# V rows of one head weighted and folded by VectorE, and an indirect load of 45 rows, in a float32 decode-attention kernel

## The chip, the cores and the metric

The kernel runs on 1 core of one Trainium2 chip. The metric is the device time in microseconds (us) of one execution; shown are the median of several runs and, for one profiled execution, the span from its first to its last instruction.

## The reference

One token's output is a gated mix of two attention blocks over caches of 8192 positions, all in float32: A with 16 heads of K and V, B with 16 query heads that share 8 heads of K and V.

```python
def _A_ref(x, k_cache, v_cache, wq, wo):          # x (1, 1, 448); caches (1, 16, 8192, 256)
    q = (x @ wq).reshape(B, Sq, 16, 256).transpose(0, 2, 1, 3)
    scores = einsum("bhqd,bhkd->bhqk", q, k_cache) * 256 ** -0.5
    o = einsum("bhqk,bhkd->bhqd", softmax(scores), v_cache)
    return o.transpose(0, 2, 1, 3).reshape(B, Sq, 16 * 256) @ wo
# _B_ref: the same, with caches (1, 8, 8192, 256), each head of which serves two query heads
g = sigmoid((x * gate_w).sum(-1, keepdims=True))
return g * _A_ref(...) + (1 - g) * _B_ref(...)
```

The caches are 402 MB of the 433 MB that are read, and each element is used once or twice.

## The kernel before

**The stream.** Everything but one part of one weight matrix is laid out ahead of time in the order of use as one stream in device memory, and SyncE loads it in 54 fills (called loads here, counted from 0) into a ring of three slots of 128 partitions x 15,936 floats. A usual load is one DMA of 15,872 columns, 7936 KB; pieces (tiles of K and V, weights) may be cut at a load's end and go on in the next. A load into a slot is issued when all readers of what stood in it are done, three loads before. `plan()` writes the order, `piece()` runs the code of each piece, and a recorder (`Seq`, whose lines 154 and 155 issue every instruction, so that nearly every row of the profile says L155) puts the instructions on their engines in the order written, with semaphore waits worked out from what overlaps.

**Sets, units, tiles.** The work is 8 sets of three units: unit (s, 2) is KV head s of B with its two query heads, (s, 0) and (s, 1) are two heads of A. Each unit has four tiles (t = 0 to 3) of 2048 positions: 128 partitions x 16 rows x 256. In the stream the V of a tile stands three K tiles after its own K (`LEAD`). So V of (s, 0) stands between K tiles of (s, 1). The query weights of set s + 1 (`wq`) come after the first of these V tiles, and the output weights of the set before (`wo`) among the first V tiles.

**Scores.** For (s, 1) and (s, 2), TensorE multiplies K against the query (`scores`, tile `sc`), VectorE takes the minimum `mn` and transposes the exponentials that ScalarE makes (`px` to `pr`). For (s, 0), K stands by rows, and VectorE does it (`scores_by_row`, the units in `BY_ROW`): a product with the query in place (`slot<-slot,qa`), a sum over each row (`sr<-slot`), the minimum over blocks of partitions (`mn`, `mt`, `st`), ScalarE's exponentials `pxr`, and then a product with `cols` that spreads the 16 weights of each partition into columns for TensorE (`pr<-pxr,cols`, line 519).

**Values.** `attend` multiplies on TensorE, two rows of V a call with 512 result columns, eight calls a tile, into a PSUM tile `o` that holds the unit's sums. `take` brings `o` to SBUF after the unit's last V tile (ScalarE and VectorE, tile `ob`), `project_o` selects the heads, and `emit_set` multiplies by `wo` into `Y`.

**Order by ticks.** `tick()` runs after each K tile and calls what is due: `gather`, `combine` (the softmax's correction factors, through a matmul into `T`, then VectorE and ScalarE, tiles `mnr`, `ew`, `es`, `z`, `rz`, `wr`), `column` (tile `sel`), `spread` (the next set's queries, `qb` and `qa`), `project_o`. All engines work in the order in which this is written.

**The indirect load.** For set 4 (`SIDE_SET`) the query weights do not all come in the stream. `SB` = 472 of B's 512 columns, for the first 384 inputs, are loaded by GpSimd's indirect DMA into the front of the slot of load 23 (`SIDE_FILL`), on 39 partitions only: `SIDE_SHARE` says how many rows each DMA engine carries, engine e serving partitions 64 * (e // 8) + 32 * h + 4 * (e % 8) + i with h in (0, 1) and i in 0 to 3. The rest of the columns (`SREST`) comes in the stream as the piece `ws`. `project_side` uses both.

Of the kernel before, what the change touches and what calls it, by code (L numbers as in the profile page):

```python
# [207 lines left out]
WQ = (4 * KF + 2) * DH  # L208
UNITS = [2, 0, 1]
BY_ROW = {(s, 0) for s in range(NS)}  # L210
KEEP = {(3, 12): 3}
LAST_CUT = [10, 6]
HEAD_AT = {2: 0, 0: 2, 1: 3}
# [2 lines left out]

SIDE_SET = 4
SIDE_FILL = 23
SIDE_SHARE = {0: 6, 2: 6, 7: 6, 8: 6, 15: 6, 4: 5, 1: 4}
SIDE_ROWS = sorted(p for e, n in SIDE_SHARE.items()  # L220
                   for p in [64 * (e // 8) + 32 * h + 4 * (e % 8) + i for h in range(2) for i in range(4)][:n])
SC8 = -(-KF * P // len(SIDE_ROWS))
SB = 472
SREST = 2 * DH - SB + 2 * DH
SIDE = SC8 * SB
XG = 2 * (KF + 1) + SC8
SLOT = 15936
# [55 lines left out]
def gated_decode_attention_kernel(  # L283
# [127 lines left out]
    ST, PR, O, GS, WR, SEL, OB, OC = ({} for _ in range(8))  # L411

    QR, SC, QA = {}, {}, {}

    def project(s, c0, w):

# [16 lines left out]
    def project_side(s, view, far):  # L433

        q = ps_s.tile([2 * BLK, 2 * DH], F32, name="sm")
        near = view[:, :KF * SREST].rearrange("p (c n) -> p c n", c=KF)
        rest = view[:, KF * SREST:]
        for a in range(2):
            nc.tensor.matmul(q[BLK * a:BLK * (a + 1), :], xz[:, KF + a, :], rest, start=True, stop=False,
                             skip_group_check=True)  # L440
        for c in range(KF):
            nc.tensor.matmul(q[0:BLK, SB:], xz[:, c, :], near[:, c, :2 * DH - SB], start=False, stop=(c == KF - 1),
                             skip_group_check=True)
            nc.tensor.matmul(q[BLK:2 * BLK, :], xz[:, c, :], near[:, c, 2 * DH - SB:], start=False, stop=(c == KF - 1),
                             skip_group_check=True)
        for c in range(SC8):
            nc.tensor.matmul(q[0:1, :SB], x8[:, c:c + 1], far[:, c * SB:(c + 1) * SB], start=False, stop=(c == SC8 - 1),
                             skip_group_check=True)
        copy_out(s, q)
# [46 lines left out]
    def scores_by_row(u, t, j0, kt):  # L496

        if t == 0 and j0 == 0:
            ST[u] = small.tile([P, 2, NT], F32, name="st", bufs=4)
        st = ST[u]  # L500
        n = kt.shape[1]
        nc.vector.tensor_tensor(kt, kt, QA[u][:, None, :].to_broadcast([P, n, DH]), op=OP.mult)
        if j0 == 0:
            SC[u, t] = small.tile([P, ROWS], F32, name="sr")
        sc = SC[u, t]
        nc.vector.tensor_reduce(sc[:, j0:j0 + n], kt, axis=AX.X, op=OP.add)
        if j0 + n < ROWS:
            return
        mn = small.tile([P, 1], F32, name="mn")
        nc.vector.tensor_reduce(mn, sc, axis=AX.X, op=OP.min)  # L510
        mt = small.tile([P, BLK], F32, name="mt")
        nc.vector.transpose(mt, mn.to_broadcast([P, BLK]))
        nc.vector.tensor_reduce(st[:, 0, t:t + 1], mt, axis=AX.X, op=OP.min)
        px = small.tile([P, ROWS // 2, 2], F32, name="pxr")
        nc.scalar.activation(px.rearrange("p q k -> p (q k)"), sc, AF.Exp, bias=st[:, 0, t:t + 1], scale=-1.0,
                             accum_out=st[:, 1, t:t + 1])
        pr = small.tile([P, NB * BLK], F32, name="pr", bufs=LEAD + 2)[:, :ROWS * NG * NT].rearrange(
            "p (q c k) -> p q c k", c=NG * NT, k=2)
        nc.vector.tensor_tensor(
            pr, px[:, :, None, :].to_broadcast([P, ROWS // 2, NG * NT, 2]),  # L520
            cols[:, t].rearrange("p g r -> p (g r)")[:, None, :, None].to_broadcast([P, ROWS // 2, NG * NT, 2]), op=OP.mult)
        PR[u, t] = pr.rearrange("p q c k -> p q (c k)")

    def attend(u, t, j0, n, vt):

        w = 2 * NG * R[heads(u)]
        if t == 0 and j0 == 0:
            O[u] = ps_o.tile([P, 2 * DH], F32, name="o")
        pr = PR[u, t]
        for j in range(j0, j0 + n, 2):  # L530
            g = j // 2 % (P // w)
            nc.tensor.matmul(O[u][w * g:w * (g + 1), :], pr[:, j // 2, :w], vt[:, j - j0:j - j0 + 2, :],
                             start=(t == 0 and j < 2 * P // w), stop=(t == NT - 1 and j >= NB - 2 * P // w),
                             skip_group_check=True)

    def take(u):

        o = O.pop(u)
        ob1 = small.tile([P, DH], F32, name="ob1", bufs=1)
        OB[u] = small.tile([P, DH], F32, name="ob", bufs=3)  # L540
        nc.scalar.activation(ob1, o[:, DH:], AF.Copy, scale=half[:, 1:2])
        nc.vector.scalar_tensor_tensor(OB[u], o[:, :DH], half[:, 0:1], ob1, op0=OP.mult, op1=OP.add)

# [14 lines left out]
    def combine(u):  # L558

        M = heads(u)  # L560
        n = NG * NT
        gi = 1 if u[1] == 2 else 0
        T = ps_s.tile([1, 2, n * M], F32, name="sm")
        nc.tensor.matmul(T, ones, GS[u].rearrange("p k g t m -> p k (g t m)"), start=True, stop=True)
        mn = small.tile([1, 2], F32, name="mnr")
        z = small.tile([1, 2], F32, name="z")
        ew = small.tile([1, 2 * n], F32, name="ew")[:, :n * M]
        es = small.tile([1, 2 * n], F32, name="es")[:, :n * M]
        nc.vector.tensor_reduce(mn[:, :M], T[:, 0, :].rearrange("p (c m) -> p m c", m=M), axis=AX.X, op=OP.min)
        for m in range(M):  # L570
            nc.scalar.activation(ew[:, m::M], T[:, 0, m::M], AF.Exp, bias=mn[:, m:m + 1], scale=-1.0)
        nc.vector.tensor_tensor(es, ew, T[:, 1, :], op=OP.mult)
        nc.vector.tensor_reduce(z[:, :M], es.rearrange("p (c m) -> p m c", m=M), axis=AX.X, op=OP.add)
        rz = small.tile([1, 2], F32, name="rz")
        nc.vector.reciprocal(rz[:, :M], z[:, :M])
        WR[u] = small.tile([1, NG // M, n, M, 2], F32, name="wr")
        for m in range(M):
            nc.vector.tensor_scalar(
                WR[u][:, :, :, m, :], ew[:, None, m::M, None].to_broadcast([1, NG // M, n, 2]),
                rz[:, m:m + 1], gate[:, gi:gi + 1], op0=OP.mult, op1=OP.mult)  # L580

    def column(u):
        M = heads(u)
        cl = ps_s.tile([P, 1], F32, name="sm")
        nc.tensor.matmul(cl, WR.pop(u).rearrange("p c x m k -> p (c x m k)"), ones[:1, :], start=True, stop=True)
        SEL[u] = small.tile([P, 2], F32, name="sel")
        if M == 2:
            nc.vector.tensor_scalar(SEL[u], which, cl, None, op0=OP.mult)
        else:
            nc.scalar.activation(SEL[u][:, :1], cl, AF.Copy)  # L590

    def project_o(u):
        M = heads(u)
        oc = ps_s.tile([P, 2, 2], F32, name="sm")
        for e in range(2):
            nc.tensor.matmul(oc[:, e, :M], OB[u][:, e::2], SEL[u][:, :M], start=True, stop=True)
        ocs = small.tile([P, 2, 2], F32, name="ocs", bufs=4)
        nc.scalar.activation(ocs[:, :, :M], oc[:, :, :M], AF.Copy)
        OC[u] = ocs
# [45 lines left out]
    def piece(kind, i, at, view):  # L645
# [17 lines left out]
        elif kind == "k":  # L663
# [5 lines left out]
            if j0 + n < 2 * NG:  # L669
                return  # L670
            tick()
            if t == NT - 1:
                gather(u)
                wait(1, combine, u)
                wait(2, column, u)
        elif kind == "v":
            u, t = TILES[i]
            n = view.shape[-1] // DH
            attend(u, t, at // DH, n, view.rearrange("p (j d) -> p j d", d=DH))
            turns = KEEP.get((len(TILES) - i, at // DH + n), 0)  # L680
            if turns:
                spare = ps_sc.tile([P, NB * BLK], F32, name="sc")
                for _ in range(turns):
                    clear(spare, NB * BLK)
            if at // DH + n == ROWS:
                if t == NT - 1:
                    take(u)
                    if u != TILES[-1][0]:
                        wait(1, project_o, u)
                if i >= len(TILES) - LEAD:  # L690
                    tick()
        elif kind == "wo" and i < NS - 1:
            emit_set(i, j0, view.rearrange("p (c n) -> p c n", c=n))
            if i == NS - 2 and j0 + n == 8:
                fold()
        else:
            for a in range(2 * NG):
                for g in range(NG):
                    b = a * D + YAT[g] - at
                    if 0 <= b < view.shape[-1]:  # L700
                        LAST[a // 2, a % 2, g] = view[:, b:b + YAT[g + 1] - YAT[g]]
# [118 lines left out]
```

## Time and profile before

| | |
|---|---|
| median of 3 runs | 1005.2 us (1004.85 to 1005.25) |
| span of the profiled execution | 1003.4 us |
| TensorE's mean granted clock in it | 0.769 |
| busy: TensorE, VectorE, ScalarE, GpSimd | 589.8, 459.2, 94.6, 4.4 us |
| read from device memory | 433.71 MB |

The profiled execution's own time is its span of 1003.4 us and what lies around it, 1.8 us to the runs' median. PE is TensorE's matmuls and PEld its weight loads, DVE is VectorE, ACT ScalarE, POOL GpSimd, and SP (SPq) the queue that issues loads. A row of a group names out<-in tiles, count, busy us and mean ns of one; a row of the chain of waits has its start, its length and what took it, for a DMA from the issue to the landing; a row of a stretch has its bounds, its length, the busy time of PE, PEld, DVE, ACT and POOL with counts, the granted clock, the share of the DMA engines and GB/s.

### The profile page before, as it was taken

Reading aid. Unit: us, or ns where it says so; the run is one execution under the profiler, and the core shown is the slowest. Engines: PE = TensorE matmul, PEld = TensorE weight load, DVE = VectorE, ACT = ScalarE, POOL = GpSimd, SP = SyncE. Lnnn points to the kernel's source line nnn. Section 1 sums busy time; section 2 is a strip of 40 time slices with the busy share of each in tenths; the row PEclk is TensorE's granted clock in tenths of the full one; section 3 lists DMA queues with packets and bytes.
Section 4 is the critical chain, followed back from the end, with each engine's and each line's share of the span. In section 5 each row is a group of like instructions: output and inputs, shape, how many; then the busy total and the mean of one; then the engine's idle time right before and its main releaser. Section 6 shows DMA issues by size and latency. Waiting matters only on the chain.

```text
span 1003.4 us, 7449 instructions
## 1 busy us (share of the span) xinstructions
PE 589.8 (59%) x3177; PEld 172.5 (17%) x3177; DVE 459.2 (46%) x651; ACT 94.6 (9%) x309; POOL 4.4 (0%) x20
## 2 busy tenths in 40 slices
PE   1745745565754654647647566545657647656448
PEld 0211211121211111112112121111212112111112
DVE  2396213961248521466214852257512485215942
ACT  0100100010100110000100011100101001100001
POOL 1000000000000000000000000000000000000000
PEclk9877877767777887877877778778677777878679
DMA  9999999999999999999999999999999999999998
GB/s 405 441 433 423 441 441 416 440 436 431 433 428 445 426 433 435 435 430 436 431 433 433 438 429 441 426 436 438 431 436 426 435 437 433 434 428 439 443 420 367
DMA packets 8963, 432.52 MB, mean 431 GB/s; under 512 B 1082, under 2 KB 1339, under 8 KB 1851
## 3 DMA queue, kind: packets, MB, share of 16 engines
q1 hardware_dynamic: 8786, 431.30, 99.4%
q0 software_dynamic: 144, 0.74, 0.2%
q8 instruction: 25, 0.41, 0.1%
q14 instruction: 8, 0.07, 0.0%
HBM read 433.71 MB, written 0.00 MB: 432 GB/s over the span
## 4 chain that ended last, share of the span: by engine, by line
DMA 70%; PE 15%; DVE 13%; ACT 1%; issue 1%; SPq 0%
DMA slot<-in_stream_dram 70%; PE o L155 7%; DVE sr L155 5%; DVE slot L155 5%; PE sc L155 5%; PE sm L155 3%; DVE pr L155 1%; DVE mn L155 1%; ACT px L155 1%; ACT pxr L155 0%; DVE st L155 0%; ACT ew L155 0%; PE Y L155 0%; DVE ob L155 0%; SPq L155 0%
## 5 line engine op out<-in xcount | busy, mean ns | idle before, releaser
L155 PE MATMUL o<-slot,pr 128*32 128x512 f32 (+1 forms) x1536 | 347.9, 759 | 221.5 <-DMA slot<-in_stream_dram 221.5
L155 PE MATMUL sc<-slot,qb 128*32 128x512 f32 x1024 | 192.3, 721 | 96.6 <-DMA slot<-in_stream_dram 96.5
L155 DVE TENSOR_REDUCE mn<-sc 128x1 f32<-128x512 f32 x64 | 44.1, 689 | 333.3 <-PE sc L155 304.5
L155 DVE TENSOR_TENSOR slot<-slot,qa 128x4096 f32<-128x4096 f32 (+7 forms) x39 | 142.4, 3652 | 44.8 <-DMA slot<-in_stream_dram 44.8
L155 PEld LDWEIGHTS o<-slot,pr 128*32 128x32 f32 (+1 forms) x1536 | 80.1, 143 | 401.5 <-DMA slot<-in_stream_dram 247.7
L155 DVE TENSOR_REDUCE sr<-slot 128x16 f32<-128x4096 f32 (+7 forms) x39 | 142.5, 3654 | 1.3
L155 ACT ACTIVATE px<-sc,st 128x512 f32<-128x512 f32 x64 | 44.0, 687 | 401.3 <-DVE st L155 401.3
L155 PEld LDWEIGHTS sc<-slot,qb 128*32 128x32 f32 x1024 | 44.8, 130 | 211.4 <-DMA slot<-in_stream_dram 111.3
L155 DVE STREAM_TRANSPOSE pr<-px 128x512 f32<-128x512 f32 x64 | 45.7, 713 | 54.1 <-ACT px L155 54.1
L155 PE MATMUL sm<-slot,xz 128*32 128x512 f32 (+2 forms) x136 | 46.1, 677 | 26.4 <-DMA slot<-in_stream_dram 19.2
L155 ACT ACTIVATE pxr<-sr,st 128x16 f32<-128x16 f32 x32 | 9.8, 307 | 376.9 <-DVE st L155 376.9
L155 PE MATMUL sm<-sel,ob 128*128 128x1 f32 (+1 forms) x96 | 18.7, 298 | 37.5 <-DVE ob L155 37.5
L155 DVE SCALAR_TENSOR_TENSOR ob<-o,half,ob 128x256 f32<-128x256 f32 x24 | 11.3, 471 | 44.5 <-ACT ob L155 44.5
L155 PEld LDWEIGHTS sm<-sel,ob 128*128 128x128 f32 x96 | 16.6, 243 | 62.3 <-DVE ob L155 54.6
L155 PEld LDWEIGHTS sm<-slot,xz 128*32 128x32 f32 (+1 forms) x136 | 11.4, 131 | 55.5 <-issue 26.4
L155 DVE TENSOR_TENSOR pr<-pxr,cols 128x256 f32<-128x256 f32 x32 | 13.6, 425 | 15.0 <-ACT pxr L155 15.0
L155 PE MATMUL Y<-slot,ocs 128*1 128x448 f32 (+1 forms) x176 | 16.7, 451 | 4.7 <-DMA slot<-in_stream_dram 4.7
L155 PE MATMUL sm<-px,spread 64*128 64x256 f32 x16 | 8.0, 594 | 13.1 <-DVE es L155 13.1
L155 ACT ACTIVATE ob<-o,half 128x256 f32<-128x256 f32 x24 | 11.3, 470 | 44.3 <-PE o L155 44.1
L155 PE MATMUL sm<-ones,wr 1*128 1x1 f32 x48 | 10.1, 277 | 7.1 <-DVE wr L155 6.9
L155 PEld LDWEIGHTS sm<-ones,wr 1*128 1x128 f32 x48 | 8.0, 208 | 30.4 <-issue 16.8
L155 ACT ACTIVATION_READ_ACCUMULATOR px<-sc,st 128x1 f32 x64 | 12.3, 193 | 0.0
(72 smaller groups left out, 154.1 us busy)
## 6 DMA issues: line engine op xcount, KB each, us to landing
slot<-in_stream_dram SPq DMA_DIRECT2D x48, 7936.0 KB, 41.2
slot<-in_stream_dram SPq DMA_DIRECT2D x1, 7840.0 KB, 47.5
slot<-in_stream_dram SPq DMA_DIRECT2D x1, 7776.0 KB, 42.9
slot<-in_stream_dram SPq DMA_DIRECT2D x1, 7680.0 KB, 20.9
slot<-in_stream_dram SPq DMA_DIRECT2D x1, 5436.0 KB, 40.9
slot<-in_stream_dram SPq DMA_DIRECT2D x1, 4864.0 KB, 35.6
slot<-in_stream_dram SPq DMA_DIRECT2D x1, 2560.0 KB, 34.4
slot<-in_stream_dram SPq DMA_DIRECT2D x1, 1280.0 KB, 33.4
```

The lines of the kernel that those rows point to most:

```text
L155: ins = getattr(engine, method)(*args, **kw)
```

## The change

For (s, 0) of sets 0 to 6 (`V_BY_ROW`) `scores_by_row` stops at the exponentials `pxr`, which are now kept for five tiles. `attend` takes VectorE: one product of the V tile (or of each of its parts where a load cuts it) in place with the weights, each repeated over its row of 256, then folds, in which rows from the upper end are added to those at the lower end until two rows are left (16 to 8 to 4 to 2). The two rows, 512 columns, are put in `held`. `release()`, called after the tick of the next K tile, multiplies each held pair on TensorE by the 16 columns of `cols` for tile t into the first 16 partitions of `o`, and after the unit's last tile calls `take` and sets `project_o` for the next tick. `take`, `combine`, `column` and `project_o` have a simpler branch for these units. Set 7 stays as it was.

The indirect load now carries all 512 columns of B's part in 9 groups of rows instead of 10, on 45 partitions: engines 9, 10 and 11 get two rows each, and a row has 18,432 B where it had 18,880. The piece `ws` is 120 columns shorter, and the first load (`xg`) one; what follows load 22 moves forward in the stream by that much. Cut to its core:

```diff
+V_BY_ROW = {(s, 0) for s in range(NS - 1)}
-SIDE_SHARE = {0: 6, 2: 6, 7: 6, 8: 6, 15: 6, 4: 5, 1: 4}
+SIDE_SHARE = {0: 6, 2: 6, 7: 6, 8: 6, 15: 6, 4: 5, 1: 4, 9: 2, 10: 2, 11: 2}
-SB = 472
-SREST = 2 * DH - SB + 2 * DH
+SB = 2 * DH
+SREST = 2 * DH
...
         for c in range(KF):
-            nc.tensor.matmul(q[0:BLK, SB:], xz[:, c, :], near[:, c, :2 * DH - SB], start=False, stop=(c == KF - 1),
-                             skip_group_check=True)
-            nc.tensor.matmul(q[BLK:2 * BLK, :], xz[:, c, :], near[:, c, 2 * DH - SB:], start=False, stop=(c == KF - 1),
+            nc.tensor.matmul(q[BLK:2 * BLK, :], xz[:, c, :], near[:, c, :], start=False, stop=(c == KF - 1),
                              skip_group_check=True)
...
-        px = small.tile([P, ROWS // 2, 2], F32, name="pxr")
+        px = small.tile([P, ROWS // 2, 2], F32, name="pxr", bufs=LEAD + 2)
...
+        if u in V_BY_ROW:
+            PR[u, t] = px.rearrange("p q k -> p (q k)")
+            return
...
+        if u in V_BY_ROW:
+            nc.vector.tensor_tensor(vt, vt, pr[:, j0:j0 + n, None].to_broadcast([P, n, DH]), op=OP.mult)
+            m = n
+            while m > 2:
+                h = m // 4 * 2
+                nc.vector.tensor_tensor(vt[:, :h], vt[:, :h], vt[:, m - h:m], op=OP.add)
+                m -= h
+            held.append((u, t, j0, n, vt[:, :2]))
+            return
...
+    def release():
+
+        for u, t, j0, n, rows in held:
+            nc.tensor.matmul(O[u][:NG * NT, :], cols[:, t].rearrange("p g r -> p (g r)"), rows,
+                             start=(t == 0 and j0 == 0), stop=(t == NT - 1 and j0 + n == NB), skip_group_check=True)
+            if t == NT - 1 and j0 + n == NB:
+                take(u)
+                wait(1, project_o, u)
+        held.clear()
...
+        if u in V_BY_ROW:
+            n = NG * NT
+            nc.scalar.activation(ob1[:n], o[:n, DH:], AF.Copy)
+            nc.vector.tensor_tensor(OB[u][:n], o[:n, :DH], ob1[:n], op=OP.add)
+            return
...
             tick()
+            release()
...
-                if t == NT - 1:
+                if t == NT - 1 and u not in V_BY_ROW:
                     take(u)
```

More of the change, by code (lines that the diff above doesn't have):

```diff
@@ L413, in gated_decode_attention_kernel @@
     QR, SC, QA = {}, {}, {}
+    held = []
     def project(s, c0, w):
@@ L575, in combine @@
         nc.vector.reciprocal(rz[:, :M], z[:, :M])
+        if u in V_BY_ROW:
+            WR[u] = small.tile([1, n], F32, name="wr1")
+            nc.vector.tensor_scalar(WR[u], ew, rz[:, :1], gate[:, gi:gi + 1], op0=OP.mult, op1=OP.mult)
+            return
         WR[u] = small.tile([1, NG // M, n, M, 2], F32, name="wr")
@@ L584, in column @@
         cl = ps_s.tile([P, 1], F32, name="sm")
+        if u in V_BY_ROW:
+            n = NG * NT
+            nc.tensor.matmul(cl[:n], WR.pop(u), ones[:1, :], start=True, stop=True)
+            SEL[u] = small.tile([P, 2], F32, name="sel")
+            nc.scalar.activation(SEL[u][:n, :1], cl[:n], AF.Copy)
+            return
         nc.tensor.matmul(cl, WR.pop(u).rearrange("p c x m k -> p (c x m k)"), ones[:1, :], start=True, stop=True)
@@ L595, in project_o @@
         for e in range(2):
-            nc.tensor.matmul(oc[:, e, :M], OB[u][:, e::2], SEL[u][:, :M], start=True, stop=True)
+            n = NG * NT if u in V_BY_ROW else P
+            nc.tensor.matmul(oc[:, e, :M], OB[u][:n, e::2], SEL[u][:n, :M], start=True, stop=True)
         ocs = small.tile([P, 2, 2], F32, name="ocs", bufs=4)
@@ L759, in apart @@
         b, a = (get(n).reshape(D, NS, 2 * DH)[:, SIDE_SET] for n in ("B_wq", "A_wq"))
-        near = _np.concatenate([b[:KF * P, SB:], a[:KF * P]], axis=1)
+        near = a[:KF * P]
         near = near.reshape(KF, P, SREST).transpose(1, 0, 2).reshape(P, KF * SREST)
         rest = _np.concatenate([b[KF * P:], a[KF * P:]])
-        return _np.concatenate([near, rest], axis=1), by_rows(b[:, :SB])
+        return _np.concatenate([near, rest], axis=1), by_rows(b)
     def col(a):
```

## The prediction

> **What bounds the kernel now.** I read the page from its top: engines, slices, DMA queues, then the chain of work that ended last.
>
> ```profile
> span 1003.4 us, 7449 instructions
> PE 589.8 (59%) x3177; PEld 172.5 (17%) x3177; DVE 459.2 (46%) x651; ACT 94.6 (9%) x309; POOL 4.4 (0%) x20
> DMA  9999999999999999999999999999999999999998
> q1 hardware_dynamic: 8786, 431.30, 99.4%
> q0 software_dynamic: 144, 0.74, 0.2%
> q8 instruction: 25, 0.41, 0.1%
> DMA 70%; PE 15%; DVE 13%; ACT 1%; issue 1%; SPq 0%
> slot<-in_stream_dram SPq DMA_DIRECT2D x48, 7936.0 KB, 41.2
> slot<-in_stream_dram SPq DMA_DIRECT2D x1, 265.0 KB, 2.8
> slot<-in_side_dram,at POOLq DMA_INDIRECT x1, 26.6
> ```
>
> No compute engine is near full, while the packets of the queues fill 99.4 + 0.2 + 0.1 = 99.7% of the time of 16 DMA engines. What is left, 0.3% of 1003.4 us, is 3 us an engine, and that is hardly more than the start and the tail. So the DMA engines are the bound, all sixteen of them, and time can only change in two ways: other bytes on the engine that ends last, or an engine that runs dry because a load was issued late. The issue row shows how far that is: a load lands 41.2 us after its issue, and 8.13 MB at 431.30 MB in 0.994 x 1003.4 us (432.4 GB/s, 27.0 an engine) take 18.8 us. So usually 22 us of queue lie ahead when the next load is issued. SyncE issues a load when its slot, of three, is consumed, so this reserve is what a later consumer eats.
>
> The compute engines' 15% and 13% in the chain are not a saving on offer: the chain steps through the slot's consumer to the next issue, while the DMA engines work on. These stretches of set 1 (its by-row K loads, what follows, then the next set) show that VectorE's load does not slow the transfers:
>
> ```profile
> 173.00:211.00 38.00, 20.81 (x76) 6.25 (x80) 35.30 (x28) 2.09 (x9) 0.00 (x0) 0.68 1.01 436
> 211.00:249.00 38.00, 24.75 (x144) 6.87 (x140) 9.54 (x23) 4.56 (x14) 0.00 (x0) 0.72 1.01 437
> 249.00:304.00 55.00, 33.91 (x184) 9.21 (x176) 19.02 (x30) 5.21 (x17) 0.00 (x0) 0.75 1.00 431
> ```
>
> The third number of each row is VectorE's busy time: 35.3 of 38 us, then 9.5 of 38, at 436 and 437 GB/s.
>
> **The DMA bytes.** The stream loses 120 columns of the weights of set 4 and one of the first load: 121 x 128 x 4 B = 62 KB, 3.9 KB an engine, -0.14 us on all. The indirect load goes from 39 rows of 18,880 B to 45 of 18,432 B: seven engines save up to 6 x 448 B (0.10 us), and engines 9, 10 and 11 get two rows each, 36.9 KB, +1.37 us. TensorE's instructions are fetched by the same engines:
>
> ```profile
> L155 PE MATMUL o<-slot,pr 128*32 128x512 f32 x1024 | 192.4, 768 | 107.2 <-DMA slot<-in_stream_dram 107.2
> L155 PE MATMUL sm<-slot,x 128*1 128x472 f32 x20 | 8.1, 559 | 0.0
> ```
>
> Ten calls of 472 columns stand as 20 records, so a call is two matmuls and two weight loads. A tile of A's V has 8 calls; 28 tiles lose 448 matmuls, their 32 pieces get back 64, the side projection loses 8: 3177 - 392 = 2785. Queue q8 moved 25 packets of 16.4 KB for 2 x 3177 instructions, one per 254; 5570 make 22, three fewer. Three fewer packets free 0.6 us (16.4 KB at 27.0 GB/s) to 1.0 us (0.15% of 16 engines' time, which rounds to the row's 0.1%, over 25) each. VectorE has 92 more instructions (below), at most one short fetch. Which engine carries which packet no view shows. If the three are on 9, 10 and 11, these end 1.37 - 0.14 - 0.6 to 1.0, so 0.2 to 0.6 us later, if they were among the last; without that, 1.2 us later; if they had slack, the end comes 0.14 to 0.24 us sooner. Bounds -0.2 to +1.2; I take +0.1, near the freed packets' lower end less some slack. The Trainium skill ("Runtime: NRT & Kernel Launch", Instruction fetch mechanics) has refills of 16 KiB, 256 instructions, "mostly hidden". The size agrees with 254 a packet; hidden they are not where DMA is the bound, and by that word the three packets would free nothing and the sum would take +1.2 here. GpSimd issues the indirect load at the same place; it landed after 26.6 us, in a slot whose own load takes about 41, so two rows more on an engine hide there, and the few matmuls that project_side saves are not on the path.
>
> **VectorE and the release of slots.** PE's saving (28 of the 64 tiles in its 192.4 us) is worth nothing by itself. What VectorE gets:
>
> ```profile
> L155 DVE TENSOR_TENSOR slot<-slot,qa 128x4096 f32<-128x4096 f32 x25 | 110.5, 4418 | 30.0 <-DMA slot<-in_stream_dram 30.0
> L155 DVE TENSOR_TENSOR slot<-slot,qa 128x2048 f32<-128x2048 f32 x2 | 4.6, 2281 | 0.0
> L155 DVE TENSOR_TENSOR slot<-slot,qa 128x1024 f32<-128x1024 f32 x2 | 2.4, 1218 | 0.0
> L155 DVE TENSOR_TENSOR slot<-slot,qa 128x512 f32<-128x512 f32 x1 | 0.7, 671 | 0.0
> L155 DVE TENSOR_TENSOR pr<-pxr,cols 128x256 f32<-128x256 f32 x32 | 13.6, 425 | 15.0 <-ACT pxr L155 15.0
> ```
>
> A tile of 16 rows: a product of 4096 (4.42 us) and folds of 2048, 1024 and 512 (2.28 + 1.22 + 0.67), with issue gaps 8.7 us; 28 tiles, 240 us. It drops pr (28 x 0.43) and with it the 0.47 us wait for ScalarE, 0.9 us a K tile. VectorE goes from 459 to about 690 us: 32 products and 88 folds come, 28 go. Over a set of about 125 us that fits. Not so in the stretch itself: a V tile of 8.7 us and the score work of the next K tile, 2.4 us, are 11.1 us for 4.19 MB that arrive in 9.7.
>
> take() of these units moves with it to the next unit's last K tile: a copy and an add of 16 rows, which nobody waits for before that set's output weights. The change also adds a wait: release() issues the folded rows' matmul only after the next K tile, in TensorE's order behind combine and spread, which wait for VectorE. A slot whose last tile is such a V tile is held into the next load. I follow set 1, whose load 9 ends in two rows of its first V tile; "load" counts slots from 0, each 18.8 us.
>
> ```profile
> 203.77 0.42 DVE L155 TENSOR_TENSOR pr<-pxr,cols 128x256 f32<-128x256 f32 x1 [0.47 <-ACT pxr L155]
> 208.98 4.42 DVE L155 TENSOR_REDUCE sr<-slot 128x16 f32<-128x4096 f32 x1
> 220.39 0.69 DVE L155 TENSOR_REDUCE mn<-sc 128x1 f32<-128x512 f32 x1 [5.33 <-PE sm L155]
> 223.43 1.22 PE sm L155 x2
> 166.61 43.84 DMA slot<-in_stream_dram
> 229.92 37.11 DMA slot<-in_stream_dram
> ```
>
> The fourth K tile ends at 213.4, less 3 x 0.9 is 210.7; its small steps and the gather take 1.4 (212.1), the V tile (2 and 14 rows) 8.4 (220.5). From the next score minimum to the end of spread's matmul it was 220.39 to 224.65, 4.3 us (224.8); two matmuls of 0.77 at half overlap and their weights, 1.0: load 12 is issued at 225.8, not at some 213.5. Load 10 landed at 166.61 + 43.84 = 210.45, load 13 at 267.03, so load 11 lands at about 229.3. Left in the queue: 3.5 us. The same steps in the other sets start here:
>
> ```profile
> 334.96 4.43 DVE sr L155
> 339.46 40.95 DMA slot<-in_stream_dram
> 458.05 0.43 DVE ob L155
> 486.84 38.99 DMA slot<-in_stream_dram
> 586.09 2.29 DVE L155 TENSOR_REDUCE sr<-slot 128x8 f32<-128x2048 f32 x1
> 597.04 41.13 DMA slot<-in_stream_dram
> 709.53 4.43 DVE sr L155
> 714.02 36.40 DMA slot<-in_stream_dram
> ```
>
> Set 2: K ends 339.4, +1.4, then three V tiles (26.1), score and combine work between (4.1 + 2.4), 1.0 for the release: 374.4; load 19 lands at 339.46 + 40.95 = 380.4; left 6.0. Set 3: the last K tile starts at 458.5, less 1.8, and takes 8.9; the same 35.0 after it: 500.6; load 26 lands 18.8 ahead of 525.8; left 6.4. Set 4: 588.4 - 1.8, and with four V tiles (34.7) and one score step more 632.7; load 33 lands at 638.2; left 5.5. Set 5: one V tile; 714.0, less 0.9 and less 1.0 for two rows of K that move into the load before, + 1.4 + 8.7 + 4.3 + 1.0: 727.5; load 38 lands at 731.6; left 4.1. Sets 0 and 6 leave more, set 7 is untouched.
>
> How much must be left? The first load (265 KB, 0.6 us of data) took 2.8 us to land: between 0 and 2.2 us of lead; I take 1. And engines do not end together: the five with six rows of the indirect load carry some 4.2 us (113 KB at 27.0 GB/s) that the rest must catch up over the span; at 230 us, half way to that load, I estimate a spread of 2 us. So the first engines have 3.5 - 2 - 1 = 0.5 us in set 1, the last 2.5. That is no stall, barely: bounds 0 to 1 us a place at five places (a gain is excluded, an early issue buys nothing); I take +0.1 in all.
>
> Sum: 1003.4 + 0.1 + 0.1 = 1003.6 us of span. The runs' median of 1005.2 us stands 1.8 above the span; **1005.4 us**.
>
> **Rivals.** *The slot comes free too late* (slower). One mechanism: the held matmul, behind VectorE's backlog. It decides from about 2 us beyond my sums in sets 1 and 5, 4 to 5 in sets 2 to 4; then each us is paid. Were each release 5 us later, the stalls after a lead of 1 us would be 2.5, 0, 0, 0.5 and 1.9 in sets 1 to 5: 5 us, 1010. For it: 11.1 against 9.7 us, and TensorE at 0.68 to 0.76 of its clock there. Against: every price is a measured row.
>
> *The product runs slower than K's* (slower): its weight is one number repeated over 256. The only row with such repeats is pr, 425 ns for 256. All of it taken as rate is 1.66 ns an element, 6.8 us a product, 2.4 more. Then sets 1 to 5 are 2.1, 7.2, 7.2, 9.6 and 2.4 us later, and beyond what is left less the lead it is 0, 2.2, 1.8, 5.1 and 0: 9 us, or 18 if the engines that are 2 us ahead count, 1014 to 1023; I say 1018. Against: pr fits the line through 512 to 4096 (0.14 us + 1.04 ns an element gives 0.41). The Trainium skill's "Vector Engine (DVE) Microarchitecture Reference" (5.2, Measured stream behaviour) has full rate only for runs of adjacent word pairs, and 1.73 ns where one source hops each element; it has no repeated word, and no run here shows one this long.
>
> *The extra rows sit on engines that were last anyway*: +1.2 us, 1006.5, no change by the measurement. *Faster* by 2 us would need idle DMA time to win; there are 3 us with start and tail.
>
> **Chances.** The forecast 0.70 (1004.8 to 1006.2), unlucky engines 0.08, late slots 0.11, slow product 0.07, faster 0.04. About 0.2% (2 us) can be told from no change: faster 0.04, same 0.78, slower 0.18. The range 1004.4 to 1009 leaves out the slow product, half of the late slots and most of faster.
>
> **What would show it.** Products near 4.42 us and folds 2.28, 1.22, 0.67; VectorE near 690 us; q8 with 22 packets; stream queue still over 99%; load 12 issued near 226, its landing near 248. A share of that queue below 99%, a wait of TensorE's held matmul beyond the times above, or a product of 6 us would make me wrong.

## The result and the profile after

The changed kernel takes **1008.18 us** (1007.59 to 1009.24), the kernel before 1005.15 us (1004.81 to 1005.27) beside it: ratio 1.0034, 95% interval 1.0024 to 1.0044. It is slower by 3.0 us, more than the 0.2% that can be told from no change. The profiled execution took 1009.22 us, with a span of 1007.8 us and a granted TensorE clock of 0.756; it stands 1.0 us above the median. Two slow executions, some 20 us longer than the others, are left out of the times below.

The same rows of the page of the changed kernel: span, engines, queues, the chain of waits by engine, and the issues of a usual load and of the indirect load.

```profile
span 1007.8 us, 6752 instructions
PE 573.4 (57%) x2785; PEld 162.8 (16%) x2785; DVE 683.2 (68%) x745; ACT 93.0 (9%) x309; POOL 4.4 (0%) x20
q1 hardware_dynamic: 8786, 431.24, 99.1%
q0 software_dynamic: 144, 0.83, 0.2%
q8 instruction: 22, 0.36, 0.1%
DMA 44%; DVE 42%; PE 10%; ACT 3%; issue 1%; SPq 0%
slot<-in_stream_dram SPq DMA_DIRECT2D x48, 7936.0 KB, 37.6
slot<-in_side_dram,at POOLq DMA_INDIRECT x1, 27.8
```

The counts are those of the change: 2785 matmuls, 22 fetch packets. The stream's share fell from 99.4 to 99.1%: 0.3% of a span of 1007.8 is 3 us in which, on the mean, an engine stood still. A usual load lands 37.6 us after its issue instead of 41.2, so the reserve in the queue has shrunk, and VectorE's share of the chain has gone from 13 to 42%: many more slots come free behind VectorE. Its new groups, with the matmul of the held rows:

```profile
L155 DVE TENSOR_TENSOR slot<-slot,pxr 128x4096 f32<-128x4096 f32 x24 | 105.5, 4397 | 0.0
L155 PE MATMUL o<-slot,cols 128*16 128x512 f32 x64 | 55.7, 974 | 100.9 <-DVE slot L155 100.9
L155 DVE TENSOR_TENSOR slot<-slot 128x2048 f32<-128x2048 f32 x24 | 55.0, 2292 | 0.8
L155 DVE TENSOR_TENSOR slot<-slot 128x1024 f32<-128x1024 f32 x30 | 36.8, 1225 | 1.0
L155 DVE TENSOR_TENSOR slot<-slot 128x512 f32<-128x512 f32 x33 | 22.8, 692 | 1.1
```

The stretches of set 1 that the prediction read (us; busy us of PE, PEld, DVE, ACT, POOL with counts; granted clock; DMA share; GB/s):

```profile
173.00:211.00 38.00, 18.33 (x71) 5.86 (x72) 35.47 (x25) 1.98 (x9) 0.00 (x0) 0.68 1.00 431
211.00:249.00 38.00, 21.27 (x86) 5.53 (x84) 34.04 (x35) 4.08 (x13) 0.00 (x0) 0.72 1.00 423
249.00:304.00 55.00, 33.96 (x186) 9.15 (x186) 25.32 (x33) 5.08 (x16) 0.00 (x0) 0.80 0.99 427
```

In the middle stretch VectorE is busy for 34.0 us instead of 9.5, and the transfers fall from 437 to 423 GB/s. The timeline shows why. First the order of K's last tiles, then the product of the V tile's two parts, then what stands ahead of the issue of load 12 (start, length, engine, instruction):

```profile
201.72 0.19 DVE L155 TENSOR_REDUCE st<-mt 128x1 f32<-128x32 f32 x1
...
202.25 0.45 ACT L155 ACTIVATE ob<-o,half 128x256 f32<-128x256 f32 x1
202.74 0.48 DVE L155 SCALAR_TENSOR_TENSOR ob<-o,half,ob 128x256 f32<-128x256 f32 x1 [0.83 <-ACT ob L155]
...
213.25 4.49 DVE L155 TENSOR_TENSOR slot<-slot,pxr 128x512 f32<-128x512 f32 x2
...
221.44 0.68 DVE L155 TENSOR_REDUCE mn<-sc 128x1 f32<-128x512 f32 x1
...
224.46 1.22 PE L155 MATMUL sm<-px,spread 64*128 64x256 f32 x2 [3.95 <-DVE es L155]
...
225.16 4.40 DVE L155 TENSOR_TENSOR slot<-slot,pxr 128x4096 f32<-128x4096 f32 x1
...
225.61 3.59 PE L155 MATMUL o<-slot,cols 128*16 128x512 f32 x4
...
227.52 0.33 SPq L155 DMA_DIRECT2D slot<-in_stream_dram  x1
```

The two rows that end load 9 are all of this V tile that load 12 waits for. Their product (512 columns, 0.68 us) is done by 213.93, but TensorE takes their held matmul at 225.61, behind spread's.

Load 12 is issued at 227.52. The packets of load 11, the last ahead of it, end by the trace's packet records between 227.33 and 227.88 on eleven of the 16 DMA engines and between 228.65 and 229.05 on the other five; the first packets of load 12 begin at 228.48. So eleven engines stood idle. The stretches around it:

```profile
215.00:227.00 12.00, 8.05 (x40) 2.80 (x37) 10.58 (x15) 2.02 (x5) 0.00 (x0) 0.78 0.99 429
227.00:230.00 3.00, 3.00 (x9) 0.77 (x11) 2.96 (x2) 0.00 (x0) 0.00 (x0) 0.57 0.96 317
230.00:233.00 3.00, 1.58 (x17) 0.46 (x9) 2.97 (x2) 0.00 (x0) 0.00 (x0) 1.00 0.80 339
```

The same happens once more, at load 39 in set 5, issued at 731.71 while load 38 lands at 734.52. There two engines were done by then, and three more before the first packet of load 39 at 732.68:

```profile
725.62 0.68 DVE L155 TENSOR_REDUCE mn<-sc 128x1 f32<-128x512 f32 x1
...
728.64 1.22 PE L155 MATMUL sm<-px,spread 64*128 64x256 f32 x2 [3.02 <-DVE es L155]
...
729.79 1.03 PE L155 MATMUL o<-slot,cols 128*16 128x512 f32 x1
...
730.62 1.06 PE L155 MATMUL o<-slot,cols 128*16 128x512 f32 x1
...
731.71 0.33 SPq L155 DMA_DIRECT2D slot<-in_stream_dram  x1
```

"Queue left" is counted from here on to the first engine's landing of the load ahead: 0.1 us at load 12, and at load 39 an engine had landed 0.5 us before the issue. Every other load is issued with more than 2 us of queue left (load 26 with 2.3, load 27 with 2.8).

One measure is used below that no view prints. Each load raises its semaphore 16 times, once per DMA engine. Against the stream's bytes at the median packet time, each increment tells how late an engine is; the zero is arbitrary, so only differences count. Each row is the one profiled execution of its version. Mean over the engines after four loads, and the first and the last engine at the end of the stream (us):

```
                         load 11  load 13  load 38  load 40  end: mean  first   last
before                     3.42     3.48     5.83     5.88      6.11     5.59    6.38
the change                 3.35     5.08     7.82     8.95      9.21     8.07   10.94
e4_fold_alone              3.30     5.16     8.15     9.89     10.07     8.86   11.96
e8_release_first_set_5     3.31     5.54     8.13     8.14      8.33     7.04    9.51
e2_release_first           3.33     3.39     5.93     5.94      6.13     4.58    7.52
e3_side_alone              3.70     3.79     6.35     6.40      6.61     5.56    8.12
e5_release_first_39        3.42     3.46     5.96     5.98      6.19     5.47    7.26
e10_no_product             3.22     3.33     5.60     5.66      5.77     4.47    6.48
e11_fetches_back           3.43     3.49     6.14     6.25      6.46     5.71    7.28
e12_rows_no_product        3.28     3.38     5.87     5.93      6.03     4.67    7.65
```

The change loses 1.7 us between loads 11 and 13 and 1.1 between 38 and 40, where the kernel before loses less than 0.1; and its engines end 2.9 us apart instead of 0.8.

### The profile page after: what moved, and what is told of

It is laid out like the page before. It is cut to its first block, busy times and chain, and to the rows that moved or that the text cites. A ratio compares the mean times of both kernels' runs of the same rounds, so it can differ in the third digit from the quotient of the medians.

```text
span 1007.8 us, 6752 instructions
## 1 busy us (share of the span) xinstructions
PE 573.4 (57%) x2785; PEld 162.8 (16%) x2785; DVE 683.2 (68%) x745; ACT 93.0 (9%) x309; POOL 4.4 (0%) x20
## 3 DMA queue, kind: packets, MB, share of 16 engines
q1 hardware_dynamic: 8786, 431.24, 99.1%
## 4 chain that ended last, share of the span: by engine, by line
DMA 44%; DVE 42%; PE 10%; ACT 3%; issue 1%; SPq 0%
DMA slot<-in_stream_dram 44%; DVE slot L155 29%; DVE sr L155 8%; PE o L155 5%; PE sc L155 3%; ACT px L155 2%; DVE mn L155 2%; PE sm L155 2%; DVE pr L155 2%; DVE st L155 1%; ACT pxr L155 1%; DVE mt L155 0%; DVE ob L155 0%; DVE wr L155 0%; ACT ew L155 0%
## 5 line engine op out<-in xcount | busy, mean ns | idle before, releaser
L155 PE MATMUL o<-slot,pr 128*32 128x512 f32 (+1 forms) x1088 | 265.6, 738 | 152.9 <-DMA slot<-in_stream_dram 152.9
L155 PE MATMUL sc<-slot,qb 128*32 128x512 f32 x1024 | 221.9, 773 | 54.0 <-DMA slot<-in_stream_dram 53.9
L155 DVE TENSOR_TENSOR slot<-slot,qa 128x4096 f32<-128x4096 f32 (+6 forms) x40 | 142.6, 3565 | 55.5 <-DMA slot<-in_stream_dram 55.4
L155 DVE TENSOR_REDUCE sr<-slot 128x16 f32<-128x4096 f32 (+6 forms) x40 | 142.7, 3567 | 1.4
L155 DVE TENSOR_TENSOR slot<-slot,pxr 128x4096 f32<-128x4096 f32 (+5 forms) x32 | 123.6, 3866 | 0.0
L155 DVE TENSOR_TENSOR slot<-slot 128x1024 f32<-128x1024 f32 (+3 forms) x88 | 116.4, 1322 | 3.0
L155 PE MATMUL o<-slot,cols 128*16 128x512 f32 x64 | 55.7, 974 | 100.9 <-DVE slot L155 100.9
L155 PE MATMUL sm<-slot,xz 128*32 128x512 f32 (+1 forms) x130 | 51.5, 758 | 47.6 <-DMA slot<-in_stream_dram 40.4
L155 PE MATMUL sm<-sel,ob 128*128 128x1 f32 (+2 forms) x96 | 17.5, 285 | 31.9 <-DVE ob L155 31.9
L155 PEld LDWEIGHTS sm<-sel,ob 128*128 128x128 f32 (+1 forms) x96 | 15.4, 226 | 53.5 <-DVE ob L155 44.1
## 6 DMA issues: line engine op xcount, KB each, us to landing
slot<-in_stream_dram SPq DMA_DIRECT2D x48, 7936.0 KB, 37.6
```

What stands on the lines that cost most here:

```text
L155: ins = getattr(engine, method)(*args, **kw)
```

## The experiments

Two theories stood against each other for the 3.0 us: late issues (two gaps in the stream, because the held matmul waits in TensorE's order), and bytes (two more rows of the indirect load on three engines). The kernel before is 1004.9 to 1005.0 us in all the comparisons below.

**Without the two late units.** The units of sets 1 and 5 go back to TensorE's values.

```diff
-V_BY_ROW = {(s, 0) for s in range(NS - 1)}
+V_BY_ROW = {(s, 0) for s in range(NS - 1) if s not in (1, 5)}
```

> Sets 1 and 5 do their first head's V on TensorE as before the change; sets 0, 2, 3, 4 and 6 keep the product and folds, and the indirect load stays at 45 rows. Theory (late slots: only the issues of loads 12 and 39 came too late, all else is hidden): the two gaps go, 1005.2 +- 0.6 us, every other load still issued with at least 2 us of queue left. Rival (VectorE's work slows the transfers or the rest in proportion): 5 of 7 sets keep their share of the 3.0 us, 1007.3. Rival (the rows on engines 9 to 11 end last): unchanged, 1008.2.

1005.97 us (1005.68 to 1006.22), ratio 1.0010 (1.0001 to 1.0019). Load 12 and load 39 have over 13 us of queue left, and 2.2 of the 3.0 us are gone with five of the seven units still on VectorE. The time lies 0.2 us above the theory's range: about 1 us over the kernel before remains.

**Release ahead of the tick.** All units stay; the held matmul is issued before the combine and spread that it stood behind.

```diff
-                wait(1, project_o, u)
+                wait(2, project_o, u)
...
+            release()
             tick()
-            release()
```

> release() is called before tick() instead of after it, so the held matmul no longer stands behind combine and spread in TensorE's order; all products and folds stay. Theory (late slots, by the order on TensorE): load 12 is issued near 223.5 instead of 227.5 and load 39 near 727.5 of a stream that is 2 us ahead, each some 4 us earlier; with 2 us of lead both are in time, 1005.2 +- 0.6 us. Rival (VectorE's work itself): 1008.2. Rival (rows on engines 9 to 11): 1008.2.

1005.92 us (1005.24 to 1007.06), ratio 1.0010 (1.0001 to 1.0019), 0.1 above the theory's range. Load 12 goes out 9 us earlier and not 4, since its pair had been ready so long; load 39 goes out 7 us earlier, of which 2.3 are the stream's (load 36 lands at 694.82 for 697.12). The two issues in its timeline, and its stretches, against those of the change:

```profile
218.44 0.33 SPq L155 DMA_DIRECT2D slot<-in_stream_dram  x1
...
724.51 0.33 SPq L155 DMA_DIRECT2D slot<-in_stream_dram  x1
```

```profile
219.00:243.00 24.00, 13.35 (x50) 3.99 (x50) 21.29 (x22) 2.25 (x7) 0.00 (x0) 0.67 1.00 431
...
723.00:747.00 24.00, 11.68 (x54) 3.31 (x58) 21.60 (x23) 2.36 (x7) 0.00 (x0) 0.63 0.99 430
```

And the changed kernel:

```profile
219.00:243.00 24.00, 11.38 (x52) 3.61 (x50) 21.56 (x23) 2.25 (x7) 0.00 (x0) 0.79 0.94 392
...
723.00:747.00 24.00, 13.54 (x60) 3.75 (x52) 21.60 (x22) 2.81 (x8) 0.00 (x0) 0.74 0.97 411
```

VectorE's work is the same in both, 21 of 24 us; only the place of one matmul differs, and 392 GB/s become 431. So the gap is the order in TensorE's queue, behind work that waits for VectorE, and not VectorE's load as such.

**The order changed in set 5 alone.** It tells what each of the two gaps costs. (In set 5 the second `release()` finds nothing held.)

```diff
-                wait(1, project_o, u)
+                wait(1 + (u[0] == 5), project_o, u)
...
+            if u[0] == 5:
+                release()
             tick()
             release()
```

> release() before tick() in set 5 alone; all else as in the change, with 45 rows. Theory (two gaps, each paid by itself): the gap at load 12 stays (2 us), that at load 39 goes: between, 1006.6 to 1007.6. Rival (the gaps do not add, the larger one or the first sets the time): 1008.2. Rival (the gap of set 5 is all of it): 1005.9.

1007.90 us (1007.10 to 1008.62), ratio 1.0029 (1.0017 to 1.0041). Its stretches:

```profile
219.00:243.00 24.00, 12.26 (x49) 3.21 (x48) 21.56 (x23) 2.25 (x7) 0.00 (x0) 0.76 0.94 389
...
723.00:747.00 24.00, 12.34 (x56) 2.98 (x50) 21.60 (x22) 2.36 (x7) 0.00 (x0) 0.78 1.01 435
```

The first gap alone costs 1007.90 - 1005.92 = 2.0 us. The second adds 0.3 (1008.18 - 1007.90) by the medians of six executions each, whose ranges overlap, and 1.3 between the two profiled ones (1009.22 and 1007.92). So the time lies above the theory's range and below the rival's value, and what the second gap costs is known only as 0.3 to 1.3 us. In the profiled execution of the change it held up the last engine too: the largest lateness of an engine goes from 9.2 at load 38 to 11.3 at load 40.

**The indirect load alone.** All V on TensorE, 45 rows.

```diff
-V_BY_ROW = {(s, 0) for s in range(NS - 1)}
+V_BY_ROW = set()
```

> Only the indirect load of 45 rows; no V by VectorE in any set, TensorE has its 8 calls a tile. Theory (late slots): no gap; engines 9 to 11 carry 1.37 us more and no fetch is freed, so up to 1.2 us over the kernel before: 1005.2 to 1006.4. Rival (VectorE's work): 1005.1. Rival (rows on engines 9 to 11 are the cost): 1008.2.

1006.05 us (1005.67 to 1006.44), ratio 1.0010 (1.0001 to 1.0019), with 25 fetch packets and no late issue. The three engines with two rows end last, at 7.79, 7.97 and 8.12 of the measure above, the next at 6.73. So the rows cost 1.1 us by themselves.

**The folds alone**, with the old load of 39 rows.

```diff
-SIDE_SHARE = {0: 6, 2: 6, 7: 6, 8: 6, 15: 6, 4: 5, 1: 4, 9: 2, 10: 2, 11: 2}
-SB = 2 * DH
-SREST = 2 * DH
+SIDE_SHARE = {0: 6, 2: 6, 7: 6, 8: 6, 15: 6, 4: 5, 1: 4}
+SB = 472
+SREST = 2 * DH - SB + 2 * DH
```

> Only the products and folds on VectorE; the indirect load is the old one of 39 rows, with the old cuts of the stream. Theory (late slots): the gaps at loads 12 and 39 stay; in set 5 K's two rows come back into load 36, so its release is some 1 us later: 1008 to 1009.5. Rival (VectorE's work): 1008.2. Rival (rows on engines 9 to 11): 1005.2.

1009.91 us (1008.65 to 1010.76), ratio 1.0046 (1.0032 to 1.0060): slower than the whole change, and above the theory's range. Its stretches:

```profile
219.00:243.00 24.00, 12.24 (x50) 3.27 (x49) 21.56 (x23) 2.25 (x7) 0.00 (x0) 0.77 0.93 392
...
723.00:747.00 24.00, 11.18 (x52) 3.42 (x50) 21.60 (x23) 2.25 (x7) 0.00 (x0) 0.79 0.97 403
```

In the table its second gap costs 1.7 instead of 1.1 us. The 120 columns that the change takes from the stream put two rows of K into the load before; back in their old place they are more for VectorE to do before load 39. Load 26 is issued with 1.4 us left instead of 2.3. So it looks as if the new rows' layout helped the releases while its bytes cost. This is a reading of one execution and not shown by a run: with the prices found elsewhere (2.0 and 0.3 for the gaps, 0.85 for VectorE's work, below) the sum is 1008.1, and some 1.8 us of this version stay without a tested cause.

**Both remedies: release first and 39 rows.** If the gaps and the rows were all, this would be the kernel before.

> release() before tick(), and the old indirect load of 39 rows with the old cuts of the stream; products and folds as in the change. Theory (the change costs two late slots and, apart from them, two rows more on each of three engines that had no slack for them): neither is left, 1004.9 +- 0.3 us, at or just below the kernel before, since three fetches of TensorE's instructions are gone. Rival (about 1 us is the price of VectorE's work, not of the rows): 1005.9.

1005.78 us (1005.39 to 1006.52), ratio 1.0008 (0.9998 to 1.0017): with neither gap nor rows some 0.9 us remain. A miss for the theory that there are two causes. Its page and its issue of load 27:

```profile
PE 579.9 (58%) x2795; PEld 162.8 (16%) x2795; DVE 682.6 (68%) x744; ACT 93.6 (9%) x309; POOL 4.4 (0%) x20
...
502.52 0.33 SPq L155 DMA_DIRECT2D slot<-in_stream_dram  x1
```

Three explanations were left: load 27 in set 3, issued at 502.52 with 1.5 us of queue left; another distribution of TensorE's fetches over the engines; and VectorE's work itself.

**Set 3 back on TensorE**, on top of the version before (`if s != 3` in `V_BY_ROW`).

> Release first, the old indirect load of 39 rows, and set 3's unit back on TensorE. What is left over the kernel before in the versions without a gap is 0.8 to 1.0 us; three theories. (a) It is the near gap at load 27 in set 3 (issued with 1.5 to 2.8 us of queue left): this version takes it away, 4 us or more are left there, and the time is 1004.9 to 1005.1. (b) It comes from which DMA engines carry TensorE's instruction fetches, of which there are fewer: 23 instead of 22, the time stays at 1005.5 to 1006.0. (c) It comes from VectorE's products and folds beside the transfers: six sevenths of them stay, 1005.6 to 1005.9.

1005.54 us (1005.15 to 1005.96), ratio 1.0005 (0.9995 to 1.0014). Load 27 now goes out at 483.90, with 20 us of queue left. That is 0.24 us less, and the interval holds the values of all three theories. The version takes away a seventh of VectorE's work together with the near gap, so it does not price the near gap by itself.

**Neither product nor folds**, on top of release first and 39 rows; the held rows are the tile's first two.

```diff
-            nc.vector.tensor_tensor(vt, vt, pr[:, j0:j0 + n, None].to_broadcast([P, n, DH]), op=OP.mult)
-            m = n
-            while m > 2:
...
```

> Release first, the old indirect load of 39 rows, and VectorE's product and folds left out: the held rows are the raw first two rows of each tile, so the weighted sum over V of these units is not computed. TensorE's instructions are as in the version with them. (a) Near gap at load 27: VectorE is done with V about 8.7 us a tile sooner, no issue is near the end of the queue, 1004.9 to 1005.1. (b) Instruction fetches: 22 packets as before, 1005.5 to 1006.0. (c) VectorE's work: its busy time falls from about 683 to about 450 us and the time to 1004.9 to 1005.1.

1004.93 us (1004.71 to 1005.27), ratio 0.9999 (0.9990 to 1.0008). From its page:

```profile
PE 560.9 (56%) x2795; PEld 160.0 (16%) x2795; DVE 446.9 (45%) x623; ACT 92.5 (9%) x309; POOL 4.4 (0%) x20
q8 instruction: 22, 0.36, 0.1%
```

TensorE has the few instructions and fetches of the change, and the time is the kernel before's. So fewer fetches neither cost nor win, and the 0.85 us come with VectorE's 236 us of work (682.6 us busy in the version with it).

Does that work slow the transfers as such? By the trace's packet records, the 6144 full packets of the stream (63,488 B) take 2.3443 us on the mean here, 2.3446 in the kernel before, 2.3446 in release first with 45 rows and all of VectorE's work, and 2.3454 in release first with 39 rows. The last is 0.4 us an engine more over the whole stream than here, of which 0.19 lies within 495 to 515 us, around load 27; with set 3 back it is gone (2.3445). So a general slowing of packets beside VectorE's work is not what these traces show.

**The fetches put back**, on top of release first and 39 rows: 14 matmuls of 8 columns of zeros behind each tile's held matmul.

```diff
+            for i in range(14 if j0 + n == NB else 0):
+                nc.tensor.matmul(O[u][:NG * NT, :8], zero[:, :NG * NT], zero[:, :8], start=False, ...)
```

> Release first, the old indirect load of 39 rows, and 14 matmuls of 8 columns of zeros behind each tile's held matmul, which add nothing to the sums and bring TensorE's instructions back to about 3177 matmuls and the fetches to 25 packets, as in the kernel before. (b) Instruction fetches: the fetches fall about as before, 1004.9 to 1005.2. (a) Near gap at load 27: it stays, and the added matmuls make the releases a little later: 1005.7 to 1006.3. (c) VectorE's work: 1005.7 to 1006.0.

1005.78 us (1005.37 to 1006.61), ratio 1.0009 (1.0000 to 1.0018), with the instructions and packets of the kernel before:

```profile
PE 584.0 (58%) x3187; PEld 171.5 (17%) x3187; DVE 683.0 (68%) x744; ACT 93.8 (9%) x309; POOL 4.4 (0%) x20
q8 instruction: 25, 0.41, 0.1%
```

The time is the same to 0.01 us. The mean of the engines ends 0.27 us later, but the last engine does not (7.28 against 7.26). A fetch packet takes 0.93 us on the mean by the trace's packet records, so three make 0.17 us on 16 engines; the rest of the 0.27 lies between two single executions and is not explained.

**The rows without VectorE's work**: release first, 45 rows, no product and folds.

> Release first, the indirect load of 45 rows as in the change, and VectorE's product and folds left out, so the weighted sum over V of these units is not computed. It holds the rows and TensorE's fewer instruction fetches (22 packets) against each other, without a late issue and without VectorE's work. The rows alone cost 1.1 us with 25 packets. If the three fetches that fall away make room on the engines with two rows each: 1005.1 to 1005.5. If they fall away elsewhere, the rows stand as before: 1005.8 to 1006.2. And for what VectorE's work costs beside the rows (version with both, no gap: 1005.9): in the first case 0.4 to 0.8 us, in the second nothing that shows, since the engines that end last are those with the rows.

1005.97 us (1004.65 to 1008.12), ratio 1.0009 (1.0000 to 1.0018). The rows cost 1.1 us with 22 fetches as they did with 25. With VectorE's work beside them (release first, 1005.92) it is no more. So the two causes do not add: each makes some engines late, and the last of them counts. In the table both end at about the mean of the kernel before (6.03 and 6.13 against 6.11), and the last engine at 7.65 and 7.52 against 6.38.

**The rows on other engines**, with release first. Engines 12, 13 and 14, then 3, 5 and 6, in place of 9, 10 and 11:

```diff
-SIDE_SHARE = {0: 6, 2: 6, 7: 6, 8: 6, 15: 6, 4: 5, 1: 4, 9: 2, 10: 2, 11: 2}
+SIDE_SHARE = {0: 6, 2: 6, 7: 6, 8: 6, 15: 6, 4: 5, 1: 4, 12: 2, 13: 2, 14: 2}
```

> release() before tick(), the indirect load of 45 rows, but the two extra rows each on engines 12, 13 and 14 instead of 9, 10 and 11. Theory (rows cost where no fetch is freed): if the three fetches that are gone were on these engines, 1004.9; if not, 1005.9 as with 9, 10 and 11; a mixture of both ends at 1005.9 too, since the last engine counts. Rival (the price of 1 us is VectorE's work): 1005.9 whatever the engines.

> The same with the extra rows on engines 3, 5 and 6. Theory (rows cost where no fetch is freed): at least one of the three places tried (9 to 11; 12 to 14; 3, 5, 6) may be free: 1004.9 if all three fetches that are gone were here, else 1005.9. Rival (VectorE's work): 1005.9 whatever the engines.

1006.13 us (1005.41 to 1007.61) and 1007.05 us (1006.42 to 1007.85), ratios 1.0013 (1.0003 to 1.0022) and 1.0021 (1.0012 to 1.0030). In the second, one engine ends at 8.94, the next at 7.49. This misses both values expected (1004.9 and 1005.9): where the rows sit matters, which the rival (VectorE's work alone) does not allow for, and why these three engines are the worst place stays open. No choice of three engines that was tried frees the load of its cost.

## Why the prediction was wrong where it was

The forecast of no change failed, and with it its step "no stall, barely": the queue ran dry at two loads. The time lies inside the stated range only because the range kept half of the rival "the slot comes free too late", whose mechanism this is; for the forecast's own sum that is luck. The account: rows and VectorE's work together 1.0 us, the gap at load 12 2.0, the gap at load 39 0.3 by the medians, which is 3.3 against 3.0 measured. These are differences of medians in a chain, so that they add up is no test; the 0.3 between comes mostly from the kernel before, which stood at 1005.15 beside the change and at 1004.9 to 1005.0 beside the experiments.

- **The counts and prices held.** Products 4.40 us (4.42 summed), folds 2.29, 1.22 and 0.69 (2.28, 1.22, 0.67), VectorE 683 us (690), 2785 matmuls, 22 packets. The rival of a slow product is refuted: 4397 ns for 4096 is 1.07 ns an element. The Trainium skill's "Vector Engine (DVE) Microarchitecture Reference" (5.2, Measured stream behaviour) has 1.73 ns where one source hops each element; a word repeated 256 times is no such case here.
- **The release of load 12's slot was summed 1.7 us too early (225.8 for 227.52).** K's end was 1.3 late: of "3 x 0.9" the first two saved 0.7 each and the third nothing, since in that tile VectorE waits 0.83 us for ScalarE's `ob` instead of for `pxr`. The small steps and the V tile took 0.4 less than summed, the steps from the score minimum to the end of spread's matmul 4.2 for 4.3. The held matmul took 1.9 (225.61 to 227.52), not 1.0, because the granted clock was 0.50 there: its two passes take 1.03 and 1.06 us and start 0.82 apart. Where the clock was 1.0, as at 233.93, a pair takes 0.60 and 0.59 us, starts 0.44 apart and is done in 1.03. So the 1.0 of the sum was the price at the full clock.
- **The lead was "between 0 and 2.2, I take 1"; it is about 2.** In the first gap load 11's packets end 0.4 us after the issue on the mean of the engines, and they lose 1.7: 2.1 in all. In the second it is 1.2 and 1.1. This decided it: 2.0 us were left for the last engine, and all of them lost time. With the lead's upper end and the 1.7 us, the sum would have had the gap: 227.5 + 2.2 is 229.7, and load 11 was summed to land at 229.3 on the last engine, 2 us sooner on the first.
- **Set 5 was 4.2 late (731.71 for 727.5)**: 2.8 because the stream was late by then, load 36 landing at 697.12 instead of 694.28; 0.6 for `ob`, less what the V tile took less; 0.9 for the held matmul. The 2.8 did not make the gap, since load 38 came as much later (734.52 for 731.6). What narrowed was the time left for the last engine, 2.8 for the 4.1 of the sum, and the first engine landed 3.4 us ahead of the last where the spread was estimated at 2 for set 1. "+0.1 in all" for the stalls was 2.3 by the medians.
- **Sets 2, 3 and 4 held**: no gap. Set 3's load 27 had 6.0 left for the last engine, by the count of the sum (6.4), but 2.8 for the first; load 26 beside it, which the sums left out, had 2.3 for the first.
- **The bytes, "+0.1, near the freed packets' lower end", were 1.1 (the indirect load alone)**, the rival of rows on engines that were last anyway, priced at 1.2. The credit for three fetches was the error: taken away or put back, they moved no median by more than 0.1 us, though each takes the 0.93 us that the prediction's bounds (0.6 to 1.0) gave it. By the Trainium skill ("Runtime: NRT & Kernel Launch", Instruction fetch mechanics) refills are "mostly hidden", which the prediction set aside; the time agrees with the page, though the packets do stand in the DMA engines' time.
- **VectorE's work costs 0.85 us where no rows are added**, a term that the sum did not have. On the medians 0.24 of it went with set 3's unit, which is both the near end of the queue at load 27 and a seventh of the work. What the rest is stays open. A general slowing of the packets is not in the traces (2.3446 us with all of the work and 2.3443 without); that leaves issues with less in reserve, or how the engines drift apart. A version with the work and early releases was not tried.

No version beats the kernel before. The DMA engines were within 0.8 us of each other there, and nothing that the change frees was the bound.

## What to carry to other kernels

Where a stream is the bound, list for every load how much queue is left when it is issued, and ask of an edit which issue comes nearest to the end: the stalls came at two loads of 54 here, and moving one call in TensorE's order took 2.3 us back without touching VectorE's work. Count bytes by the last DMA engine, not by the mean: two edits that each make some engines 1 us late cost 1 us together, and bytes saved elsewhere pay nothing.

## What was not expected of the hardware

- After a gap a load does not start at once. Issued at 227.52, its first packets begin at 228.48, 0.96 us later, and take 2.5 to 3.6 us instead of 2.34, where nearly all engines start together; the last engine begins at 230.40, 1.3 us after any of them had ended the load before. At 731.71 the first began at 732.68, the last at 735.34, where all had been done by 734.21. The packet records do not name the engine, so how long a single one waited is not shown. On the mean of the engines the first gap is 0.9 us of standing still and 0.7 of longer first packets.
- TensorE's held matmul, 512 columns in two passes, has one of two prices, and its mean of 974 ns a pass hides them: of the 64 passes, 53 ran wholly or nearly so at a granted clock of 0.5 and took 1016 to 1061 ns, ten ran at 1.0 and took 592 to 603, and one that saw the clock change took 816. The 768 ns of the calls with `pr` is a mean of this kind too.
- VectorE's work in the slots does not slow the stream's packets in general: 2.3446 us a packet with 683.7 us of VectorE's work (release first, 45 rows), 2.3443 with 446.9 (no product and folds, 39 rows).
